# Pooling v in three parts, one routing group for the last nine tiles, and routing operations on both sides of the normalisation

## The chip, the cores and the metric

The kernel runs on one core of a Trainium2 chip. The metric is the device time of one execution in microseconds (us). TensorE (PE) multiplies matrices, VectorE (DVE) and ScalarE (ACT) work on elements, GpSimd (POOL) does element work and issues the indirect DMAs, SyncE (SP) issues most other DMAs. Every engine works through its own queue in order.

## The reference

Three layers follow one another. Only the first two touch the change.

```
k_p = mean of k over 8 neighbours;  v_p likewise             # 8 batches, 8 heads, 576 x 64
attn = softmax(q @ k_p.T / 8);  x = attn @ v_p               # x: 4608 tokens x 512
do   = x @ w_skip > 0;  logits = x @ w_gate                  # 8 experts
e    = argmax(logits);  gate = softmax(logits)[e]
out  = x + gate * (relu(x @ w1[e]) @ w2[e])   where do, else x
y    = (h * sigmoid(h)) @ w_out,  h = out @ w_in             # 2048 wide
```

## The kernel before, in words

**Attention** goes over 36 tiles of 128 tokens. A batch has 576 tokens, so two batches make nine tiles and the middle one of the nine belongs to both. `first[b]` is the first tile of batch b: 0, 4, 9, 13, 18, 22, 27, 31. In pass i of the loop the engines get, in the order of the code: the score products of tile i+3 (`products`, tile name `s`), the transposes of the probabilities of tile i+1 (`ptrans`, `pt` and its copy `pts`), the row maxima and exponentials of tile i+3 (`mx` on VectorE, `prb` on ScalarE), the product with v of tile i (`pv`), and the normalisation of tile i (`post`). There is one PSUM tile for `pv`, so the product of tile i+1 can start only when `post` of tile i has read it. `post` is five VectorE operations: `sm` (add), `sm` (reciprocal), `cc`, `x`, `lg`; `x` is the last but one and the last to read the PSUM tile. `lg` holds the router's logits and the skip score; they come out of `pv` as extra columns, since the router's weights are applied to the pooled v in advance.

**Pooling v.** `pool_v(b)` adds the eight neighbours on GpSimd in three additions (1280, 640 and 320 elements per partition; tile names `v`, `v`, `vp`). In passes with i + 2 = first[b] it is called for batch b+1, all three additions in one pass, from b = 1 on. `router1(b+1)` transposes `vp` on TensorE (`vtp`) three passes later, in pass first[b]+1; `values(b+1)` copies it to its place (`vex`) in the same pass, and `router2` applies the router's weights (`cps`) two passes after that.

**Routing** works on groups of tiles. `GROUP` names five: three of nine tiles, one of six (27 to 32) and one of three (33 to 35). When the last tile of a group has been normalised, `route` appends two steps to a list, and each later pass takes one entry from it. `step1` is eight VectorE operations that end with the one-hot choice `roh`, `rohb` and with `sb`. `count` is one TensorE product and one more per tile (`rps`) and reads `rohb`; it stands in TensorE's queue in front of that pass's `pv`. `step2` is nine VectorE operations that end with the slot numbers `ix`. Then one indirect DMA per tile, issued by GpSimd, scatters the token numbers into a list in DRAM (`slots<-consts,ix`). These scatters are paced: at most one is placed at the start of a pass, behind ScalarE's last instruction, and one at its end, behind VectorE's last instruction. The start one is left out in passes before 18 when three or fewer are waiting.

**The order of VectorE's work in a pass.** The code first exhausts the routing step of this pass (`a`), except in the last two passes, then takes four operations of `self.slow` (`keep_one`, sixteen small operations, from pass 30 on), then pools a part of a later batch's k, and then does `post`, taking one leftover operation of `a` after each of its operations. Passes 30 to 33 also subtract a quarter of the first expert's weights (`w1l`).

**After attention** the last group is routed within the first expert unit: `step1`, two blocks of the first product (`hp`), `count`, `step2`, all of the group's scatters at once, then the work list (`units`, small VectorE operations) beside the blocks that follow. GpSimd then reads the whole token list back (`table<-slots`), behind all scatters. VectorE's `taken` (`table<-table,sc`) waits for it; behind `taken` in VectorE's queue stand the copy `xr`, the last `hl` and the low parts of the second half of the first expert's second weights (`w2l`), which TensorE needs from the fifth block of the second product (`yp`) on. The gather of the next unit's tokens waits for `taken` too. A loop over the other units follows, then the third layer.

An order of issue is fixed per engine by the code, with one exception: the scatters are tied only to their own data and to the instruction that paces them, and the planner may put one ahead of an addition of `pool_v` that was written before it; what is written after a scatter on GpSimd stays behind it.

Of the kernel before, what the change touches and what calls it, by code (L numbers as in the profile page):

```python
# [5 lines left out]
F32 = mybir.dt.float32  # L6
# [7 lines left out]
ALU = mybir.AluOpType  # L14
AX = mybir.AxisListType
# [3 lines left out]
P = 128  # L19
B, H, S, D = 8, 8, 576, 64  # L20
# [5 lines left out]
NTILE = NT // P  # L26
CP, NC = 120, 5
# [15 lines left out]
KEYS = {2: (2, 3, 4, 4), 3: (6, 6, 7, 8), 4: (11, 12, 13, 13), 5: (15, 15, 16, 17), 6: (20, 20, 21, 22),  # L43
        7: (24, 24, 25, 26)}
DEEP = 3
LAST = 32
FMIN = float(np.uint32(0x38100000).view(np.float32))
PACE = [3, 3, 3, 3, 1, 0] + [3, 2, 3] * 5
HALF = 6
# [2 lines left out]
ON0, ON1 = 3,0  # L52
OPS = [2, 2, 2, 0, 4, 4]
ORDER = list(range(NT // 512))[::-1]
SLOW = 4
A1, A2, A3 = 8, 12, 12

C_E, C_MV, C_LID, C_WT, C_THR, C_LE, C_UN, C_PK, C_TRI = 0, 2, 13, 49, 57, 153, 217, 241, 265
# [30 lines left out]


GROUP = {}
for _g, (_t0, _n) in enumerate([(0, 9), (9, 9), (18, 9), (27, 6), (33, 3)]):
    GROUP.update({_t0 + _j: (_g, _j, _n) for _j in range(_n)})


# [62 lines left out]
class Kern:  # L158
# [19 lines left out]
    def attention(self, xa, rs, extra):  # L178
        nc, tc, c = self.nc, self.tc, self.c
        self.todo = todo = []  # L180
        self.slow = iter(())
        with tc.tile_pool(name="as", bufs=1) as s1, \
# [16 lines left out]
            q_t, k_t, v_t, st = {}, {}, {}, {}  # L199
# [10 lines left out]
            def loadq(b):  # L210
                q_t[b] = s2.tile([P, 4, S], F32, name=f"q{b}", tag="q", bufs=3)
                nc.sync.dma_start(q_t[b], self.qT[b])
# [11 lines left out]
                    eng.tensor_tensor(k[:, :, :, 0:2], k[:, :, :, 0:2], k[:, :, :, 2:4], ALU.add)  # L224
                    eng.tensor_tensor(kp, k[:, :, :, 0], k[:, :, :, 1], ALU.add)

            def pool_v(b, on_dve=0):

                v, g, n = v_t.pop(b), nc.gpsimd, on_dve
                vp = st[b, "v"] = s2.tile([P, NC, D], F32, name=f"vp_{b}", tag="vp")  # L230
                if n:
                    nc.vector.tensor_reduce(vp[:CP, 0:n], v[:CP, 0:n].rearrange("p c t d -> p c d t"), AX.X, ALU.add)
                v, vp = v[:CP, n:], vp[:CP, n:]
                g.tensor_tensor(v[:, :, 0:4], v[:, :, 0:4], v[:, :, 4:8], ALU.add)
                g.tensor_tensor(v[:, :, 0:2], v[:, :, 0:2], v[:, :, 2:4], ALU.add)
                g.tensor_tensor(vp, v[:, :, 0], v[:, :, 1], ALU.add)

            def values(b):
                vp, ve = st[b, "v"], vex[b % NB]
# [44 lines left out]
            def products(t):  # L284
                pss = []
                for a in range(2):
                    ps = bank(f"s_{t}{a}")
                    for b, o, r, m in parts(t):
                        for hp in range(2):
                            nc.tensor.matmul(ps[r:r + m, 144 * hp:144 * hp + 144], q_t[b][:, 2 * a + hp, o:o + m],  # L290
                                             kbd[b % NB][:, 2 * a + hp].rearrange("p a g -> p (a g)"),
                                             start=True, stop=True)
                    pss.append(ps)
                return pss
# [60 lines left out]
            first = [9 * (b // 2) + 4 * (b % 2) for b in range(B)]  # L355
# [27 lines left out]
            for i in range(-2, NTILE):  # L383
                if i == -2:
                    pool_v(0, ON0)
                if i > DEEP and i + 3 < NTILE:
                    pss = products(i + 3)
                    pts[i + 1] = ptrans(i + 1, prs.pop(i + 1))
                    prs[i + 3] = scores(i + 3, pss)
                elif i != -1 and i <= DEEP:  # L390
                    prs[i + 2] = scores(i + 2)
                if len(self.to_place) > (3 if i < EARLY else 0) and i < NTILE - 1:
                    self.place(1, nc.scalar.last)
                extra(i, True)
                ready = todo.pop(0) if todo and i < NTILE - 1 else None
                if ready and ready[0]:
                    ready[0]()
                if i == -2:
                    values(0)
                    loadv(1)  # L400
                    loadq(1)
                if i == -1:
                    pss = products(1)
                    router1(0)
                if i == 0:
                    pv(0, pts.pop(0))
                if 0 <= i + 1 < NTILE and i + 1 not in pts:
                    pts[i + 1] = ptrans(i + 1, prs.pop(i + 1))
                if i == -1:
                    prs[1] = scores(1, pss)  # L410
                    router2(0)
                    pool_k(1, nc.vector, (0,))
                    pool_v(1, ON1)
                    values(1)
                if i > 0:
                    pv(i, pts.pop(i))
                a = ready[1]() if ready and ready[1] else iter(())
                b = post(i) if i >= 0 else iter(())
                for _ in range(99 if i < LAST else ready[2] if ready and i < NTILE - 2 else 0):
                    next(a, None)  # L420
                for _ in range(SLOW):
                    next(self.slow, None)
                for bb, tiles in KEYS.items():
                    for r, t in enumerate(tiles):
                        if i == t:
                            pool_k(bb, nc.vector, (r,), 1)
                for _ in b:
                    next(a, None)
                for _ in a:
                    pass  # L430
                for bb, tiles in KEYS.items():
                    if i == tiles[-1]:
                        keys(bb)
                if i == 0:
                    pool_k(1, nc.vector, (2,))
                    keys(1)
                for b in range(B):
                    if i + 4 == first[b] and 0 < b < B - 1:
                        loadq(b + 1)
                    if i + 2 == first[b]:  # L440
                        if 0 < b < B - 1:
                            pool_v(b + 1)
                        if b + 2 < B:
                            loadk(b + 2)
                            loadv(b + 2)
                    if i + 2 == first[b] + 3 + (b == 0) and b + 1 < B:
                        router1(b + 1)
                    if i + 2 == first[b] + 3 and 0 < b < B - 1:
                        values(b + 1)
                    if i + 2 == first[b] + 5 and b + 1 < B:  # L450
                        router2(b + 1)
                if i == DEEP:
                    prs[i + 3] = scores(i + 3)
                if i == EARLY + 7:
                    self.read_table(nc.sync)
                if i == 2:
                    nc.sync.dma_start(self.cb, self.con[:, P + C_TRI:])
                if i == 6:
                    self.consts()
                if i < NTILE - 1:  # L460
                    self.place(1, nc.vector.last)
                else:
                    self.place(len(self.to_place))
                extra(i)
# [1174 lines left out]
```

## Time and profile before

| | |
|---|---|
| time, median of 3 runs | 1295.41 us (1293.82 to 1295.55) |
| the profiled execution: its time, its span | 1300.88 us, 1299.1 us |
| TensorE, VectorE, ScalarE, GpSimd busy in the span | 96%, 66%, 44%, 27% |
| attention (score products to last `pv`) | about 9.7 to 152.2 us |
| first expert unit (first `hp` to last `yp`) | 152.8 to 193.8 us |

The profile was taken from one execution; its span runs from the first to the last instruction. A row of a timeline gives the start and the duration in us, the engine, the code line (a helper's, so the same in all rows), the operation, output <- inputs by tile names, the shape and the count; in square brackets stands the idle time of the engine before it and what ended that. A pass is found by its `pv`.

### The profile page before, as it was taken

Reading aid. Unit: us, or ns where it says so; the run is one execution under the profiler, and the core shown is the slowest. Engines: PE = TensorE matmul, PEld = TensorE weight load, DVE = VectorE, ACT = ScalarE, POOL = GpSimd, SP = SyncE. Lnnn points to the kernel's source line nnn. Section 1 sums busy time; section 2 is a strip of 40 time slices with the busy share of each in tenths; the row PEclk is TensorE's granted clock in tenths of the full one; section 3 lists DMA queues with packets and bytes.
Section 4 is the critical chain, followed back from the end, with each engine's and each line's share of the span. In section 5 each row is a group of like instructions: output and inputs, shape, how many; then the busy total and the mean of one; then the engine's idle time right before and its main releaser. Section 6 shows DMA issues by size and latency. Waiting matters only on the chain.

```text
span 1299.1 us, 20276 instructions
## 1 busy us (share of the span) xinstructions
PE 1244.8 (96%) x6469; PEld 1059.0 (82%) x6470; DVE 851.4 (66%) x1559; ACT 576.7 (44%) x1224; POOL 352.9 (27%) x313
## 2 busy tenths in 40 slices
PE   6998887999989989999999999999999999999998
PEld 5988767998878979887788888788888888888887
DVE  5887785666776768888724245556784657847565
ACT  5877534445565445443433334424344243533321
POOL 5476532122222212212456502111111010210100
PEclk9999998999999999999999999999999999999999
DMA  9887526565565633347664323553546343463532
GB/s 379 302 302 266 195 82 221 176 208 185 209 208 186 232 107 123 138 165 265 235 214 159 130 90 117 199 176 124 167 163 213 131 169 119 155 214 113 178 114 90
DMA packets 94187, 234.43 MB, mean 180 GB/s; under 512 B 15077, under 2 KB 26981, under 8 KB 90400
## 3 DMA queue, kind: packets, MB, share of 16 engines
q1 hardware_dynamic: 86816, 216.47, 48.2%
q0 software_dynamic: 7008, 16.80, 4.0%
q8 instruction: 42, 0.69, 0.2%
q14 instruction: 33, 0.27, 0.1%
q10 hardware_dynamic: 288, 0.20, 0.0%
HBM read 183.24 MB, written 52.89 MB: 182 GB/s over the span
## 4 chain that ended last, share of the span: by engine, by line
PE 60%; DVE 1%; issue 1%; DMA 1%; ACT 0%; SPq 0%; DVEq 0%; ACTq 0%
PE yb L115 21%; PE ps L115 17%; PE fh L115 9%; PE fop L115 9%; PE hp L115 1%; PE yp L115 1%; PE fxp L115 1%; DMA wout<-wdo 0%; DVE fr L115 0%; PE sx L115 0%; DVE ft L115 0%; DVE fsg L115 0%; DMA out<-fo 0%; ACT fgh L115 0%; DVE fgl L115 0%
## 5 line engine op out<-in xcount | busy, mean ns | idle before, releaser
L115 PE MATMUL yb<-wout,g 128*128 128x512 f32 x1152 | 268.4, 391 | 0.8 <-DMA wout<-wdo 0.8
L115 PEld LDWEIGHTS yb<-wout,g 128*128 128x128 f32 x1152 | 215.0, 188 | 45.7 <-DMA wout<-wdo 0.9
L115 POOL TENSOR_TENSOR tm<-tm,tm 128x512 f32<-128x512 f32 x24 | 32.2, 1343 | 411.9 <-ACT tm L115 411.9
L115 DVE TENSOR_TENSOR yacc<-yb,yacc 128x512 f32<-128x512 f32 x168 | 116.1, 691 | 38.7 <-PE yb L115 31.4
L115 ACT COPY tm<-ps 128x512 f32<-128x512 f32 x72 | 42.4, 589 | 146.2 <-PE ps L115 144.4
L115 ACT CAST g<-sg 128x512 fp32r<-128x512 f32 x96 | 59.6, 620 | 76.9 <-DVE sg L115 76.9
L115 DVE TENSOR_TENSOR fsg<-fh,fsg 128x512 f32<-128x512 f32 x48 | 33.1, 689 | 85.7 <-ACT fsg L115 85.7
L115 ACT ACTIVATE hh<-hp 128x256 fp32r<-128x256 f32 (+1 forms) x96 | 39.4, 411 | 105.8 <-PE hp L115 97.2
L115 DVE TENSOR_TENSOR w2l<-raw,w2h 128x512 fp32r<-128x512 f32 x96 | 65.9, 692 | 28.9 <-ACT w2h L115 23.9
L115 PE MATMUL hp<-xth,w1h 128*128 128x256 f32 (+2 forms) x384 | 72.9, 313 | 12.1 <-issue 8.3
L115 PE MATMUL yp<-w2l,hh 128*128 128x512 f32 x208 | 81.2, 390 | 3.0 <-DVE w2l L115 3.0
L115 PE MATMUL fh<-w1l,fh 128*128 128x512 f32 x336 | 83.4, 390 | 0.0
L115 PE MATMUL yp<-w2h,hh 128*128 128x512 f32 x208 | 83.3, 400 | 0.0
L115 PE MATMUL yp<-w2h,hl 128*128 128x512 f32 x208 | 81.3, 391 | 0.0
L115 DVE TENSOR_TENSOR tm<-ps,tm 128x512 f32<-128x512 f32 x24 | 16.6, 691 | 98.1 <-PE ps L115 98.1
L115 PE MATMUL hp<-xtl,w1h 128*128 128x256 f32 (+2 forms) x384 | 72.3, 309 | 2.0 <-DVE xtl L115 1.9
L115 PEld LDWEIGHTS fh<-w1l,fh 128*128 128x128 f32 x336 | 62.8, 188 | 12.9
L115 PEld LDWEIGHTS hp<-xth,w1h 128*128 128x128 f32 x384 | 61.1, 195 | 14.0 <-issue 12.9
L115 PE MATMUL hp<-xth,w1l 128*128 128x256 f32 (+2 forms) x384 | 71.3, 308 | 0.0
L115 ACT ACTIVATE prb<-s,mx 128x72 f32<-128x72 f32 x288 | 65.6, 357 | 9.5 <-DVE mx L115 9.3
L115 PE MATMUL fop<-fh,fgh 128*128 128x512 f32 x168 | 66.4, 395 | 3.2 <-ACT fgh L115 3.2
L115 ACT ACTIVATE fsg<-fh 128x512 f32<-128x512 f32 x48 | 28.7, 599 | 91.6 <-PE fh L115 91.6
(240 smaller groups left out, 2756.2 us busy)
## 6 DMA issues: line engine op xcount, KB each, us to landing
raw<-w SPq DMA_DIRECT2D x88, 512.0 KB
wout<-wdo SPq DMA_DIRECT2D x48, 512.0 KB
win<-wdi SPq DMA_DIRECT2D x36, 512.0 KB
w1l<-wdi SPq DMA_DIRECT2D x36, 512.0 KB
xa<-x SPq DMA_DIRECT2D x36, 256.0 KB
fx<-xa SPq DMA_DIRECT2D x9, 1024.0 KB
v<-vR SPq DMA_DIRECT2D x7, 1280.0 KB
fr<-w_in SPq DMA_DIRECT2D x16, 512.0 KB
```

The lines of the kernel that those rows point to most:

```text
L115: ins = f(*a, **k)
```

## The change

The last nine tiles (27 to 35) become one routing group. `pool_v(b+1)` does one of its three additions in each of the passes first[b]-2, first[b]-1 and first[b], instead of all in the first of them. In every pass five operations of the routing step are issued ahead of the k pooling and of `post`, and the rest of them after `post`. `self.slow` gives two operations in a pass instead of four, and four in the last two passes.

```diff
-LAST = 32
+FILL = 5
-SLOW = 4
+SLOW = 2
-for _g, (_t0, _n) in enumerate([(0, 9), (9, 9), (18, 9), (27, 6), (33, 3)]):
+for _g, (_t0, _n) in enumerate([(0, 9), (9, 9), (18, 9), (27, 9)]):
...
-            def pool_v(b, on_dve=0):
-
-                v, g, n = v_t.pop(b), nc.gpsimd, on_dve
-                vp = st[b, "v"] = s2.tile([P, NC, D], F32, name=f"vp_{b}", tag="vp")
-                if n:
-                    nc.vector.tensor_reduce(vp[:CP, 0:n], v[:CP, 0:n].rearrange("p c t d -> p c d t"), AX.X, ALU.add)
+            def pool_v(b, on_dve=0, steps=(0, 1, 2)):
+                v, g, n = v_t[b], nc.gpsimd, on_dve
+                vp = st.get((b, "v"))
+                if vp is None:
+                    vp = st[b, "v"] = s2.tile([P, NC, D], F32, name=f"vp_{b}", tag="vp")
+                    if n:
+                        nc.vector.tensor_reduce(vp[:CP, 0:n], v[:CP, 0:n].rearrange("p c t d -> p c d t"), AX.X,
+                                                ALU.add)
                 v, vp = v[:CP, n:], vp[:CP, n:]
-                g.tensor_tensor(v[:, :, 0:4], v[:, :, 0:4], v[:, :, 4:8], ALU.add)
-                g.tensor_tensor(v[:, :, 0:2], v[:, :, 0:2], v[:, :, 2:4], ALU.add)
-                g.tensor_tensor(vp, v[:, :, 0], v[:, :, 1], ALU.add)
+                for j in steps:
+                    if j < 2:
+                        m = 4 >> j
+                        g.tensor_tensor(v[:, :, 0:m], v[:, :, 0:m], v[:, :, m:2 * m], ALU.add)
+                    else:
+                        g.tensor_tensor(vp, v[:, :, 0], v[:, :, 1], ALU.add)
...
-                for _ in range(99 if i < LAST else ready[2] if ready and i < NTILE - 2 else 0):
+                for _ in range(FILL):
                     next(a, None)
-                for _ in range(SLOW):
+                for _ in range(SLOW if i < NTILE - 2 else 2 * SLOW):
                     next(self.slow, None)
...
                 for _ in b:
-                    next(a, None)
+                    pass
                 for _ in a:
                     pass
...
+                    if 0 <= i + 2 - first[b] < 3 and 0 < b < B - 1:
+                        pool_v(b + 1, 0, (i + 2 - first[b],))
                     if i + 2 == first[b]:
-                        if 0 < b < B - 1:
-                            pool_v(b + 1)
                         if b + 2 < B:
```

## Rows read from the trace of the kernel before

**Rows 1.** The page: busy time (share of the span) and instructions of each engine.
```profile
PE 1244.8 (96%) x6469; PEld 1059.0 (82%) x6470; DVE 851.4 (66%) x1559; ACT 576.7 (44%) x1224; POOL 352.9 (27%) x313
```
**Rows 2.** Windows, passes 28 to 33: length, busy us (instructions) by engine, clock, DMA share, GB/s.
```profile
122.00:147.00 25.00, 20.82 (x171) 18.73 (x169) 23.52 (x94) 18.70 (x66) 13.99 (x16) 1.00 0.72 239
```
**Rows 3.** Waits of TensorE from 15 to 154 us: total, times, longest.
```profile
PE pv L115 <- DVE x L115: 7.6, 10, 2.1
```
**Rows 4.** Timeline of TensorE: the products with v of tiles 33, 34, 35.
```profile
143.08 1.63 PE L115 MATMUL pv<-vex,pts 120*128 120x148 f32 x10 [1.65 <-DVE x L115]
...
147.46 1.63 PE L115 MATMUL pv<-vex,pts 120*128 120x148 f32 x10 [0.84 <-DVE x L115]
...
150.65 1.61 PE L115 MATMUL pv<-vex,pts 120*64 120x148 f32 x20 [0.91 <-DVE ri L115]
```
**Rows 5.** Timeline of VectorE, passes 30 and 33: slow operations, routing step 1, start of normalisation.
```profile
133.25 0.15 DVE L115 TENSOR_TENSOR sc<-m,tot 1x8 f32<-1x8 f32 x1
...
133.71 0.15 DVE L115 TENSOR_SCALAR sm<-pv 128x8 f32<-128x8 f32 x1
...
144.17 0.20 DVE L115 TENSOR_REDUCE rmx<-lg 128x6 f32<-128x48 f32 x1
...
146.06 0.15 DVE L115 TENSOR_SCALAR sm<-pv 128x8 f32<-128x8 f32 x1
```
**Rows 6.** Timeline of VectorE, passes 18 and 19: a group of nine.
```profile
86.64 0.25 DVE L115 TENSOR_TENSOR roh<-req,rm 128x72 f32<-128x72 f32 x1
...
87.16 0.16 DVE L115 TENSOR_SCALAR sm<-pv 128x8 f32<-128x8 f32 x1
...
88.52 0.82 DVE L115 TENSOR_REDUCE mx<-s 128x4 f32<-128x288 f32 x2
89.25 0.16 DVE L115 TENSOR_TENSOR tot<-tot,rps 128x8 f32<-128x8 f32 x1
...
90.90 0.16 DVE L115 TENSOR_SCALAR sm<-pv 128x8 f32<-128x8 f32 x1
```
**Rows 7.** Timeline of TensorE, pass 19: the count and the product behind it.
```profile
87.67 0.38 PE L115 MATMUL rps<-rohb,onesb 128*128 128x72 bf16 x9
88.57 1.63 PE L115 MATMUL pv<-vex,pts 120*128 120x148 f32 x10 [0.52 <-DVE x L115]
```
**Rows 8.** Timeline of GpSimd, pooling v of batch 4.
```profile
63.12 2.94 POOL L115 TENSOR_TENSOR v<-v 120x1280 f32<-120x1280 f32 x1
66.22 1.00 POOL L115 DMA_INDIRECT slots<-consts,ix  x1 [0.17 <-DVE vex L115]
...
68.88 0.87 POOL L115 TENSOR_TENSOR vp<-v 120x320 f32<-120x320 f32 x1
```
**Rows 9.** Timeline of TensorE, pass 14: the transposes that read this `vp`.
```profile
71.45 0.47 PE L115 MATMUL vtp<-ident,vp 120*128 120x120 f32 x3
```
**Rows 10.** Timeline of GpSimd after attention: scatters and the table read.
```profile
163.49 0.98 POOL L115 DMA_INDIRECT slots<-consts,ix  x1 [4.00 <-DVE ix L115]
164.77 0.98 POOL L115 DMA_INDIRECT slots<-consts,ix  x1 [0.30 <-issue]
...
168.72 0.60 POOL L115 DMA_DIRECT2D table<-slots  x1 [1.68 <-DMA slots<-consts,ix]
```
**Rows 11.** Timeline of VectorE after attention.
```profile
161.05 0.56 DVE L115 SCALAR_TENSOR_TENSOR hl<-hp,hh 128x384 fp32r<-128x384 f32 x1 [3.69 <-ACT hh L115]
...
174.41 0.17 DVE L115 TENSOR_TENSOR sc<-table,m 128x24 f32<-128x24 f32 x1
```
**Rows 12.** Windows: the last stretch in which the table's bytes move; a later half-clock stretch.
```profile
482.60:486.40 3.80, 3.80 (x12) 3.80 (x13) 3.31 (x5) 1.71 (x2) 1.25 (x1) 0.50 0.20 74
...
170.50:171.00 0.50, 0.50 (x4) 0.28 (x2) 0.46 (x3) 0.04 (x1) 0.00 (x0) 1.00 0.18 65
```
**Rows 13.** Timeline of TensorE: two products behind a wait.
```profile
177.24 0.50 PE L115 MATMUL yp<-w2l,hh 128*128 128x512 f32 x1 [1.82 <-DVE w2l L115]
...
482.55 1.62 PE L115 MATMUL hp<-xth,w1h 128*128 128x384 f32 x4 [3.81 <-PEq L1635]
```

## The prediction

> **What bounds the kernel now.** I read the page first: TensorE is busy for 96% of the span [rows 1], so a microsecond counts only where TensorE waits or is pushed back. The change lies in the first 195 us, so I went on with the waits of TensorE over attention. What the reader sees there is that it waits mostly for one thing, the normalisation `x` of the tile before: 7.6 us in ten waits [rows 3]. The windows by stage show why at the end of attention: from 122 to 147 us VectorE is busy 23.5 of 25 us and TensorE 20.8 [rows 2], so there VectorE sets the pace, while before that TensorE does. The timelines of TensorE, VectorE and GpSimd then give the places, and I followed the first expert unit up to the loop. There TensorE waits twice for VectorE's low parts `w2l`, the second time 1.82 us [rows 13], behind VectorE's table work. All sums below are differences within the profiled execution (1300.88 us, span 1299.1); I add them to the median of the plain runs, 1295.41 us, which is 5.5 us lower than the profiled one.
>
> **Part 1: the last tiles lose a routing group.** Four slow operations take 0.46 us before the normalisation (133.25 to 133.71) [rows 5]. Two instead of four save 0.23 us in each of passes 30, 31 and 32, where VectorE is full [rows 2], so tile 33's product starts some 0.7 us earlier, at 142.4 instead of 143.08 [rows 4]. In pass 33 step 1 of the six-tile group and four slow operations lie from 144.17 to 146.06, 1.89 us, ahead of the normalisation [rows 5]; of that 0.23 stays. Then what is late next is TensorE: product, normalisation, product. That cycle is 3.19 us between tiles 34 and 35 (147.46 to 150.65), where step 2 was interleaved with it [rows 4]; without step 2 I put it at 3.1, against 4.38 from tile 33 to tile 34. Tile 34 comes at 145.5 and tile 35 at 148.5, 2.1 us earlier than now, and step 2's end no longer delays the last split of x, which adds a little: **-2.3 us** when the expert unit starts. Bounds: -1.4 (step 1's own 1.89 less 0.46) and -2.9 (0.7 and the whole 2.2 of the two shorter cycles). The eight slow operations that move to passes 34 and 35 cost nothing while VectorE waits there for the product; without that cover they cost 0.5 us a pass. One of two logit stores leaves SP's queue and the other grows to nine tiles; the weight loads behind it are first read after the table's arrival, so I count nothing, and 0.5 us if they came late.
>
> **Part 2: routing operations on both sides of the normalisation.** Five operations of step 1 now come first, and `roh`, `rohb` and `sb` after the normalisation. In pass 18 these three take 0.52 us (86.64 to 87.16) and the normalisation 1.36 us (87.16 to 88.52) [rows 6]. So `x` is ready 0.5 us earlier, but `rohb` only at 88.5 instead of before 87.2. The count reads it, takes 0.38 us, and stands in TensorE's queue in front of the product of tile 19 [rows 7]. Behind that waiting count are this product and the whole next pass. The count would run from 88.6 to 89.0, the product start there instead of at 88.57: 0.4 us later where it should have been 0.5 us earlier. In the next pass four of step 2's nine operations (1.65 us in all, 89.25 to 90.90 [rows 6]) move behind the normalisation, which pays about a third of this back. I count +0.25 and +0.3 us for the first two groups and nothing for the third, which lies where VectorE is full and the order doesn't change its sum: **+0.55 us**. Bounds: -1.6 (the third part of 7.6 us that stands in routing passes outside the tail, an estimate from [rows 3] of two waits a group) and +1.2 (three counts late by 0.4).
>
> **Part 3: v in three parts.** GpSimd runs its queue in order, and in passes with paced scatters a part that is written after a scatter stays behind it. Now one scatter lies between the first addition (63.12) and the end of `vp` (69.75) [rows 8]. With the additions in passes 11, 12 and 13, four lie between: the end of pass 11, start and end of pass 12, start of pass 13. A scatter takes 1.28 us from start to start (163.49 to 164.77) [rows 10]; three more are 3.85 us, and `vp` is ready at 73.6. The transposes that read it stand in TensorE's queue at 71.45 [rows 9]: 2.2 us too early. Behind them wait the next tile's scores and everything after. The same pattern stands a second time, with batch 6 in pass 23; the other four batches are pooled where no scatter is waiting. A mean wait for `x` is 0.76 us [rows 3], and one such wait at each place is swallowed by the late start, so I take 2.2 - 0.76 = 1.45 twice: **+2.9 us**. Bounds: 0, if the planner lets the additions go ahead or GpSimd is early, and +5.0, if nothing is swallowed and the scatters of pass 13 wait for their pacer a little longer. What GpSimd has gained by then (scatters that come out earlier) nobody waits for.
>
> **Part 4: nine scatters after attention instead of three.** The scatters follow `ix`, one every 1.28 us, and the table read waits for the last: 168.72 us [rows 10]. Six more are 7.7 us. A count of ten products instead of four adds 0.25 us; step 2 on nine tiles takes 1.65 us [rows 6], and with three it fills 161.6 to the first scatter at 163.49 less its latency, about 1.6, so it adds nothing. The table's bytes have moved by 171.0 [rows 12], and VectorE takes the table at 174.4 without a wait [rows 11]; allowing 0.4 us for the signal, 3.0 us of the delay are hidden. Left are 7.7 + 0.3 - 3.0 = **+5.0 us**. Behind the waiting VectorE operation stand the copy `xr`, which the next unit's gather waits for, the last `hl`, and the four `w2l` that TensorE already waits for at 177.24 [rows 13]; from there to the loop VectorE's chain has no room of that size, and the loop starts from its end. Bounds: +2.6, if the 3.69 us in which VectorE waited before 161.05 [rows 11] shrink to what the count then sets (2.4 us less), and +8.0, if the signal came only just in time.
>
> **Part 5: the clock in that wait.** TensorE's wait before the fifth block grows from 1.82 us [rows 13] to nearly 7. [...] From the rows I take about half, **+1.0 us**, since VectorE's own chain runs on beside those products and the adds wait for it; bounds 0 and +1.9.
>
> **Sum:** -2.3 + 0.55 + 2.9 + 5.0 + 1.0 = +7.15, and 1295.41 + 7.15 = **1302.6 us**.
>
> **The rivals.** A: the v parts are in time (the planner orders the scatters late). For it: in the rows a scatter was put ahead of an addition, so the order is the planner's; against: what is written after a scatter can't pass it. Then +4.25, 1299.7 us. B: the 3.69 us gap of VectorE doesn't come back, so the scatters start 2.4 us earlier. For it: TensorE's block that ScalarE waited for had long ended; against: nothing of the change lies in it. Then +4.75, 1300.2 us; with A as well, 1297.3. C, the other side: the normalisation's lead takes away every wait of TensorE for `x`, 7.6 us [rows 3], in place of parts 1 and 2, with v in time. Against the 6.0 us of parts 4 and 5 that leaves -1.6, 1293.8 us, faster or the same. It decides from 6 us of waits on. For it: it is the largest wait of the stage; against: the longest, 2.1 us, is behind a pooling of k, which stays ahead of the normalisation, and the count needs what is put behind it.
>
> **How the numbers follow.** A change of 0.2%, 2.6 us, is about what a measurement of this kernel can tell from none. Chances: the forecast 0.50, A 0.20, B 0.12 (with or without A), C 0.10, something else 0.08. Slower by over 2.6 us: 0.47 of the forecast, 0.15 of A, 0.09 of B and 0.03 of the rest, 0.74. Within: 0.03, 0.05, 0.03, 0.06 of C and 0.03, 0.20. Faster: 0.06. The likeliest case's own range, with the bounds of its parts, is 1299.5 to 1305.5; the range for all is 1297.0 to 1306.0, which leaves out C and the far ends.
>
> **What would show it.** Right: nine scatters in a row after attention, the table read some 5 to 6 us later behind the first `hp`, and TensorE idle near 7 us inside the first `yp` block, followed by a clock of 0.5; transposes `vtp` that wait for `vp` in passes 14 and 23; counts that wait for `rohb`; tiles 33 to 35 at 3.1 us each. Wrong: `vtp` without a wait (A), first scatter within 2 us of the count (B), or tiles before 122 us closer together than now (C). The prediction fails as a whole if VectorE reaches `taken` and finds the table there.

## The result and the profile after

The changed kernel takes 1305.4 us (median of 6), the kernel before 1296.0 beside it: ratio 1.0087, 95% interval 1.0070 to 1.0104. That is 9.4 us slower by the medians and some 11 by the ratio. The side was right; 1302.6 was too little. The profiled execution took 1309.89 us, span 1307.8, and was the slowest of the six. TensorE is busy 4.1 us more than in [rows 1], but only 0.8 more than in a second trace of the kernel before (e5 below: 1248.1 us busy, span 1291.8), while the span is 16.0 longer than there. Against that trace nearly all of the loss is waiting:
```profile
PE 1248.9 (95%) x6468; PEld 1063.5 (81%) x6469; DVE 851.1 (65%) x1542; ACT 577.6 (44%) x1224; POOL 356.5 (27%) x313
```
Attention first. Timelines of TensorE and GpSimd, after: the transposes of the pooled `v`, four scatters inside the pooling [rows 8, 9], the counts behind `rohb` [rows 7], and the last three tiles 3.08 us apart [rows 4]. The waits for `x` fall from 7.6 us in ten [rows 3] to 3.5 in four (in e5 they are 4.9 in eight).
```profile
74.96 0.53 PE L115 MATMUL vtp<-ident,vp 120*128 120x120 f32 x3 [2.20 <-POOL vp L115]
108.69 0.53 PE L115 MATMUL vtp<-ident,vp 120*128 120x120 f32 x3 [1.54 <-POOL vp L115]
...
57.14 0.21 PE L115 MATMUL rps<-rohb,trib 128*128 128x72 bf16 x1 [0.43 <-DVE rohb L115]
90.87 0.21 PE L115 MATMUL rps<-rohb,trib 128*128 128x72 bf16 x1 [0.55 <-DVE rohb L115]
128.82 0.19 PE L115 MATMUL rps<-rohb,trib 128*128 128x72 bf16 x1 [1.37 <-DVE rohb L115]
...
143.54 1.63 PE L115 MATMUL pv<-vex,pts 120*128 120x148 f32 x10 [1.12 <-DVE x L115]
146.62 1.63 PE L115 MATMUL pv<-vex,pts 120*128 120x148 f32 x10 [0.91 <-DVE x L115]
```
```profile
64.61 2.93 POOL L115 TENSOR_TENSOR v<-v 120x1280 f32<-120x1280 f32 x1
67.70 0.99 POOL L115 DMA_INDIRECT slots<-consts,ix  x1 [0.17 <-issue]
...
73.03 0.99 POOL L115 DMA_INDIRECT slots<-consts,ix  x1 [0.30 <-ACT prb L115]
74.01 0.90 POOL L115 TENSOR_TENSOR vp<-v 120x320 f32<-120x320 f32 x1
```
Then the tail. GpSimd after: nine scatters, the eighth 3.27 us long, and the table read [rows 10].
```profile
160.17 0.98 POOL L115 DMA_INDIRECT slots<-consts,ix  x1 [7.03 <-DVE ix L115]
161.46 0.98 POOL L115 DMA_INDIRECT slots<-consts,ix  x1 [0.30 <-issue]
...
169.16 3.27 POOL L115 DMA_INDIRECT slots<-consts,ix  x1 [0.30 <-issue]
172.74 0.98 POOL L115 DMA_INDIRECT slots<-consts,ix  x1 [0.30 <-issue]
175.41 0.60 POOL L115 DMA_DIRECT2D table<-slots  x1 [1.69 <-DMA slots<-consts,ix]
```
VectorE after [rows 11]: its subtractions stand beside that scatter, and it now waits for the table.
```profile
169.10 2.48 DVE L115 TENSOR_TENSOR w2l<-raw,w2h 128x512 fp32r<-128x512 f32 x4
...
177.91 0.18 DVE L115 TENSOR_TENSOR table<-table,sc 128x24 f32<-128x24 f32 x1 [5.89 <-DMA table<-slots]
```
TensorE after [rows 13]: the wait for `w2l`, the wait ahead of the loop's first product (8.26 us in the trace read before the prediction), and the one at its exit; then windows with the granted clock [rows 12].
```profile
180.59 0.80 PE L115 MATMUL yp<-w2l,hh 128*128 128x512 f32 x1 [7.74 <-DVE w2l L115]
208.51 1.27 PE L115 MATMUL hp<-xth,w1h 128*128 128x256 f32 x4 [10.19 <-issue]
491.03 1.62 PE L115 MATMUL hp<-xth,w1h 128*128 128x384 f32 x4 [6.00 <-PEq L1640]
```
```profile
182.10:186.30 4.20, 4.20 (x11) 3.25 (x10) 2.99 (x18) 1.24 (x2) 1.01 (x1) 0.50 0.60 162
186.30:192.00 5.70, 5.70 (x30) 4.78 (x28) 5.38 (x7) 1.19 (x2) 0.39 (x1) 0.99 0.00 0
```
The traces of the chips on which the kernel before takes 1293 to 1296 us, side by side, in us, worked out from the timelines. Attention: first product with v to the first product of the first expert unit (the "first FFN product" of the expectations). Table, last: from that product to VectorE's second operation on the table, and to the end of the unit's last product. Entry: TensorE's wait ahead of the loop's first product. Loads: start of the loads for the fourth block of the third layer (the "fourth FFN block" of the expectations), ahead of the last product's end. The traces of e9 to e16, from two other chips, follow with their experiments.
```
                     attention  table  last   entry  loads
before (rows 1-13)    133.9    21.8   41.0    8.3    1.5
before again (e5)     131.1    20.2   39.5    6.2    1.5
after                 131.6    26.0   46.5   10.2    3.2
after again (e1)      133.2    26.2   46.7   10.9    3.2
after again (e17)     133.2    26.1   45.2    6.8    1.8
group only (e2)       128.3    26.1   46.4   10.1    3.0
parts only (e3)       134.3    20.2   39.7    5.8    1.5
order only (e4)       131.8    20.3   39.6    7.1    1.5
six in the tail (e6)  133.1    20.1   39.5    6.1    1.5
sub ahead (e7)        131.5    28.1   46.9    7.4    1.5
sub behind (e8)       133.2    23.8   45.2    7.0    1.5
late loads (e18)      131.5    26.0   46.3    6.6    1.4
```
The same kernel's attention differs by 1.7 to 2.7 us from trace to trace, so its total can't weigh smaller effects. But product by product these traces agree within 0.05 us over long stretches, so it can be said where a difference lies: the first trace of the kernel before starts tile 28 4.2 us later than e5, counted from the first product with v, and e2, e4 and e6 start it within 0.1 us of e5. The columns table and last repeat within 1.5 us for equal code, but for the first row, which stands apart.

### The profile page after: what moved, and what is told of

It is laid out like the page before. It is cut to its first block, busy times and chain, and to the rows that moved or that the text cites. A ratio compares the mean times of both kernels' runs of the same rounds, so it can differ in the third digit from the quotient of the medians.

```text
span 1307.8 us, 20248 instructions
## 1 busy us (share of the span) xinstructions
PE 1248.9 (95%) x6468; PEld 1063.5 (81%) x6469; DVE 851.1 (65%) x1542; ACT 577.6 (44%) x1224; POOL 356.5 (27%) x313
## 4 chain that ended last, share of the span: by engine, by line
PE 60%; DVE 1%; issue 1%; DMA 1%; ACT 0%; SPq 0%; DVEq 0%; ACTq 0%
PE yb L115 21%; PE ps L115 17%; PE fop L115 10%; PE fh L115 9%; PE hp L115 2%; PE yp L115 1%; PE fxp L115 1%; DMA wout<-wdo 0%; PE sx L115 0%; DVE fsg L115 0%; DVE fr L115 0%; DMA out<-fo 0%; ACT fgh L115 0%; DVE fgl L115 0%; DVE ft L115 0%
## 5 line engine op out<-in xcount | busy, mean ns | idle before, releaser
L115 ACT ACTIVATE hh<-hp 128x256 fp32r<-128x256 f32 (+1 forms) x96 | 39.5, 411 | 108.2 <-PE hp L115 101.7
L115 ACT ACTIVATE prb<-s,mx 128x72 f32<-128x72 f32 x288 | 65.5, 354 | 10.7 <-DVE mx L115 10.7
L115 DVE TENSOR_TENSOR g<-sg,g 128x512 fp32r<-128x512 f32 x96 | 65.8, 686 | 5.4 <-ACT g L115 5.0
```

Source lines behind the costliest of these rows:

```text
L115: ins = f(*a, **k)
```

## The experiments

Ratios are to the kernel before in the same set of runs, with 95% intervals.

**e1, no edit (after).** 

> The changed kernel unaltered, beside the three that follow. Two waits of TensorE that nothing in the diff explains are longer in its trace than in the one before: ahead of the loop's first product (10.19 us against 8.26) and at the loop's exit (6.00 against 3.81), 4.1 us of the 8.7 by which the spans differ. Theory T1 (they belong to the program, or follow from the longer table path): both stand here within 0.3 us of 10.2 and 6.0, and the ratio to the kernel before is 1.0085 to 1.0095. Rival T2 (they vary from execution to execution): at least one is over 1 us nearer to the kernel before's.

1.0085 (1.0062 to 1.0109), entry 10.9, exit 4.95: the entry wait repeats, the exit does not.

**e2, the group alone.**
```diff
-... [(0, 9), (9, 9), (18, 9), (27, 6), (33, 3)]
+... [(0, 9), (9, 9), (18, 9), (27, 9)]
```


> The kernel before with one edit: its last nine tiles are one routing group. T1 (the nine scatters with the table behind them are the main loss): the table is used 3 to 5 us later after the start of the first FFN block than before (15.7 us there: 158.3 to 174.6 less the block's start), the half-clock stretch follows, passes 33 to 35 give back up to 2, and the time is up by 3 to 6 us, ratio 1.0023 to 1.0046. Rival T3 (the order of the routing operations and the late transposes are the main loss): under +1.5 us, ratio below 1.0012. Of the loop's two waits: if they hang on the longer table path they are long here too (10 and 6 us), otherwise about 8.3 and 3.8.

1.0041 (1.0026 to 1.0056), +5.3 us: attention 2.8 shorter, everything behind it worse, the entry long too. Up to tile 33 its products with v start within 0.03 us of e5's; from tile 33 to tile 35 they are 6.15 us apart where e5's are 9.00. T1 holds, T3 falls. TensorE:
```profile
177.09 0.80 PE L115 MATMUL yp<-w2l,hh 128*128 128x512 f32 x1 [7.77 <-DVE w2l L115]
204.72 1.22 PE L115 MATMUL hp<-xth,w1h 128*128 128x256 f32 x4 [10.06 <-issue]
```
**e3, the parts alone** (`pool_v` and its call as in the change). 

> The kernel before with one edit: v pooled in parts in three passes. T1: the transposes of the pooled v in passes 14 and 23 wait for GpSimd's last addition 1.5 to 2.2 us, the net is 0.3 to 1.5 us each, and the time is up by 1 to 3 us, ratio 1.0008 to 1.0023. Rival T3: since the normalisation of before's order keeps those passes short of VectorE anyway, the two waits hide in the waits for x, and the ratio is 0.9995 to 1.0005. The loop's two waits as in the kernel before (8.3 and 3.8 us) if they hang on the table path.

1.0017 (1.0001 to 1.0032), +2.2 us: T1, though the interval reaches into T3's 0.9995 to 1.0005. The waits stand where they were forecast, and are not hidden: tile 28 starts 4.6 us later than in e5.
```profile
73.90 0.53 PE L115 MATMUL vtp<-ident,vp 120*128 120x120 f32 x3 [1.89 <-POOL vp L115]
109.18 0.53 PE L115 MATMUL vtp<-ident,vp 120*128 120x120 f32 x3 [1.54 <-POOL vp L115]
```
**e4, the order alone** (`FILL = 5`, `SLOW = 2` and the loops that use them). 

> The kernel before with one edit: five routing operations ahead of the normalisation in every pass and the rest behind it, two of the one-row operations in place of four. T1: the waits of the value products for x in passes 10, 11, 19, 20 go (about -0.5 us each), waits of the count products for rohb come (0.4 to 1.4 us), passes 33 to 35 lose less to the one-row operations (up to -1.5 us), and the time moves by -2 to +1 us, ratio 0.9985 to 1.0008. Rival T3 (the order is the main loss): over +2 us, ratio above 1.0015.

1.0001 (0.9989 to 1.0012): T1; the order by itself costs nothing measurable.

**e5, no edit (before).** 

> The kernel before unaltered, for a second trace of it: the execution whose trace was read took 1300.88 us, 5 above the median. Theory T5 (those 5 us lie in the gaps of passes 14 to 25 and at the loop's entry, and are of that execution): here the stretch from the first value product to the first product of the FFN is 1.5 to 4 us shorter than the 133.85 read, the wait ahead of the loop's first product is 5.8 to 7.1 us as in the two kernels with one edit and three tail scatters, and the span is 1293 to 1296. Rival T6 (they are the program's, and the edits take them away): 133.9, 8.3 and 1299.

1.0000 (0.9987 to 1.0013), span 1291.8. T5 holds with 131.1 and 6.2; the span is a little under its 1293. The 3.69 us gap of VectorE [rows 11] belonged to that execution too: here the first scatter comes 8.4 us after the first FFN product, in the changed kernel 8.3, in the trace of rows 10 10.7. The tail is compared with this trace from here on. GpSimd and TensorE:
```profile
159.45 0.98 POOL L115 DMA_INDIRECT slots<-consts,ix  x1 [1.71 <-DVE ix L115]
...
166.57 0.60 POOL L115 DMA_DIRECT2D table<-slots  x1 [3.56 <-DMA slots<-consts,ix]
```
```profile
173.93 0.50 PE L115 MATMUL yp<-w2l,hh 128*128 128x512 f32 x1 [1.73 <-DVE w2l L115]
196.77 1.22 PE L115 MATMUL hp<-xth,w1h 128*128 128x256 f32 x4 [6.24 <-issue]
```
**e6, six in the tail.**
```diff
-... (18, 9), (27, 6), (33, 3)]
+... (18, 9), (27, 3), (30, 6)]
```


> The kernel before with its last nine tiles as groups of three and six: six scatters in the tail in place of three or nine, five groups as before. T1 with a threshold (the table path counts only from where it outlasts the products): the scatters end some 6 us earlier after the first FFN product than with nine, before the eighth's place beside the four subtractions, the table is used 19.5 to 21 us after the first FFN product (20.3 with three, 26.1 with nine), TensorE's wait for w2l stays at 1 to 2 us, the full clock holds and the entry wait is 6 to 8: ratio 0.999 to 1.001. Rival T7 (every scatter more in the tail costs the same, a sixth of what six cost): half of the 9 to 10 us of tail and entry that nine cost over three, +4.5 us, ratio 1.0035.

1.0013 (1.0000 to 1.0025). Table 20.1, last 39.5, wait for `w2l` 1.71: three more scatters cost the tail nothing, six more cost 7 us. It is a threshold, T7 falls. The trace's loss lies in attention, where the waits for `x` are 8.7 us in all against 4.9 in e5, the longest 3.3 in front of tile 33's product.

**e7, subtractions ahead of the table** (in the changed kernel).
```diff
+mm1(U * P, (7,), False)
+for f in range(4, 8):
+    low2(f)
 self.taken()
...
-mm1(U * P, (7,), False)
-for f in range(4, 8):
-    low2(f)
```


> The changed kernel with the last four subtractions of the second weights' low part, and the FFN block that they need, issued ahead of the two operations on the table. T1 (the table's lateness costs by way of VectorE, which stands at the table with those subtractions behind it): TensorE's wait of 7.7 us ahead of the fifth block's low product and the half clock behind it go, the last product of the stage ends 7 to 9 us earlier after the first FFN product than 46.5, the entry wait falls to 6 to 8 us, and the time falls to 1295 to 1299, ratio 0.999 to 1.0025. Rival T8 (the gather behind the table is what counts): the wait moves to the transposes of the gathered rows and 4 us or more of it stay, ratio above 1.005. More of VectorE's subtractions stand beside the scatters here: if those lengthen them (T4), more than one scatter is longer than 1.2 us.

1.0074 (1.0054 to 1.0094): T8, not T1. The wait for `w2l` goes (0.21 us), and the gathered rows are late in its place, 5.3 and 0.9 us; and now two scatters are long. GpSimd, VectorE and TensorE:
```profile
168.94 3.27 POOL L115 DMA_INDIRECT slots<-consts,ix  x1 [0.30 <-issue]
172.52 2.94 POOL L115 DMA_INDIRECT slots<-consts,ix  x1 [0.31 <-issue]
```
```profile
168.88 2.48 DVE L115 TENSOR_TENSOR w2l<-raw,w2h 128x512 fp32r<-128x512 f32 x4
172.10 2.47 DVE L115 TENSOR_TENSOR w2l<-raw,w2h 128x512 fp32r<-128x512 f32 x4
```
```profile
186.35 0.48 PE L115 MATMUL xtp<-ident,xn 128*128 128x128 f32 x1 [5.31 <-DMA xn<-xa,gi]
```
**e8, subtractions behind the table** (in the changed kernel).
```diff
-for f in range(4):
-    low2(f)
 ...
 self.taken()
+for f in range(4):
+    low2(f)
```


> The changed kernel with the first four of those subtractions moved behind the table's two operations, so that no subtraction stands beside the scatters. T4 (a VectorE operation with two inputs lengthens the scatter that it meets): the eighth scatter takes 0.98 us instead of 3.27 and the table is used 2.0 to 2.4 us earlier (23.7 to 24.1 us after the first FFN product instead of 26.1). Rival T9 (the eighth scatter is long for a reason of its own, such as the number of scatters under way): it stays at 3.2 us. TensorE is the worse for it in either case, since it stands from the first block's low product on: 2 to 3 us of products that ran ahead of the wait now run behind it, so that under T4 the time is within 1 us of the changed kernel's, ratio to before 1.0075 to 1.0095, and under T9 2 to 3 us above.

1.0060 (1.0040 to 1.0081). T4 holds: the eighth scatter takes 0.98 us and the table comes 2.3 us earlier. The time was better than T4's 1.0075; the entry wait is short in this trace (7.0 us), which may be why.
```profile
169.70 0.98 POOL L115 DMA_INDIRECT slots<-consts,ix  x1 [0.30 <-issue]
170.99 0.98 POOL L115 DMA_INDIRECT slots<-consts,ix  x1 [0.30 <-issue]
```
e9 to e16 ran on two other chips, where the kernel before takes 1300.7 and 1301.9 us.

**e9, e10, e12: groups of 9, 9, 12 and 6** (`(18, 12), (30, 6)`, two tiles widened), in the kernel before, in the changed one, and in the kernel before with the new order. 

> The kernel before with four routing groups of 9, 9, 12 and 6 tiles in place of five of 9, 9, 9, 6 and 3: one group fewer, as in the change, but six scatters in the tail, which cost the table nothing. T1: the table is used 20 to 20.5 us after the first FFN product, the last product of the stage ends at 39.5 and the entry wait is 6 to 7, all as in the kernel before; the attention from the first value product on is 1 to 2.8 us shorter than 131.1 (128.3 with 9, 9, 9 and 9); ratio 0.9978 to 0.9992. Rival T11 (the twelve scatters of the third group and the one-row operations behind it, all in the last six passes, take that back there): attention 131 to 133, ratio 1.000 to 1.0015.

> The changed kernel with groups of 9, 9, 12 and 6 tiles in place of 9, 9, 9 and 9: the parts of v and the order of the routing operations stay, six scatters stand in the tail in place of nine. T1 (the nine scatters carry the loss, in the tail and at the loop's entry): TensorE waits 1.7 us for w2l in place of 7.7, the last product ends 39.5 us after the first FFN product in place of 46.5, the entry wait is 6 to 7 in place of 10 to 11, and 10 us of the 11 go: ratio 0.999 to 1.0025. Rival T3 (order and parts together cost more than each by itself): ratio above 1.004.

> The kernel before with groups of 9, 9, 12 and 6 tiles and with the changed order of the routing operations, v pooled whole. T1: as the run with the groups alone, and the order moves it by -1 to +1 us (it was +0.1 us by itself, interval -1.4 to +1.6); with two one-row operations to a pass in place of four, those behind the third group run on into the FFN and lie behind VectorE's first work there: ratio 0.998 to 0.9998. Rival T11: above 1.0005, with TensorE's waits for x in passes 31 to 35 over 4 us in all.

1.0045 (1.0030 to 1.0060), 1.0032 (1.0018 to 1.0045), 1.0047 (1.0032 to 1.0063). None gains. In e9 and e12 T11 has the side right, but its size is far off: attention is 141.5 us in e9 where it said 131 to 133, while the waits for `x` in e12's passes 31 to 35 are 3.5 us where it said over 4. How much of that is the third group's work in the last passes isn't shown, for in all three traces ScalarE also stands 5.0 to 5.7 us there, and TensorE 2.9 to 3.1, for a releaser that the profile calls remote. TensorE of e9:
```profile
157.90 2.34 PE L115 MATMUL pv<-vex,pts 120*64 120x148 f32 x20 [2.92 <-remote]
```
In e10 the waits for `w2l` are down to 0.6 and 1.8 and the entry to 7.3, as T1 has it, but attention is 137.5, and the ratio lies between T1's 1.0025 and T3's 1.004, with an interval that reaches into both.

**e11, a quarter of the loads.**
```diff
-self.load_w1(e)
+nc.sync.dma_start(self.raw1[:, 0], self.row(self.w1, e)[0:P, :])
```


> The changed kernel, with three of the four loads of an expert's first weights left out at the top of the loop (the loop's units compute with rows that are not the expert's). Only the wait ahead of the loop's first product is read. T10 (an instruction fetch stands behind those loads in the DMA queues, since they start 0.6 us behind the stage's last product there and the fetch comes behind them): with a quarter of the bytes the wait falls from 10.2 to 10.9 us to 4 to 7. Rival T12 (the fetch is late by itself, whatever the loads): 9.5 us or more.

One run. The entry was 7.18 us, but the wait for `w2l` was 4.81 for another reason (below), and other kernels with whole loads have 7 there too: inconclusive.

**e13, the fourth block's loads late.**
```diff
-self.ffn_load(3)
...
+self.xtrans((2, 3))
+self.ffn_load(3, behind=nc.vector.last)
```


> The changed kernel with one thing moved: the two loads for the fourth FFN block wait for VectorE's last split of the gathered rows. In the traces with the long entry wait (10.1 to 10.9 us) these loads start 3.0 to 3.2 us ahead of the stage's last product and the first instruction fetch of queue q8 comes 1 to 2 us behind that product; in the traces with a short one (5.8 to 8.3) they start 1.5 us ahead, and the fetch comes 1 to 2 us ahead of the product. T10 (the fetch stands behind those loads in the DMA queues): with the loads at 1.4 to 1.6 us ahead the fetch comes ahead of the product again, the wait falls to 6 to 8 us although TensorE still waits 7.7 us for w2l and the clock is halved, and the time falls by 2 to 4 us against the changed kernel, ratio to before 1.0055 to 1.007. Rival T12 (the fetch is late because TensorE is): the wait stays at 9.5 us or more, ratio 1.008 to 1.0095.

0.9986 (0.9968 to 1.0004), outside the ranges of both theories, with a wait for `w2l` of 4.82 us, so it did not tell T10 from T12. It showed something else: ScalarE stands still ahead of the last blocks, VectorE's subtractions come behind the scatters, and no scatter is lengthened. ScalarE, VectorE and GpSimd:
```profile
174.45 0.49 ACT L115 ACTIVATE hh<-hp 128x384 fp32r<-128x384 f32 x1 [4.07 <-remote]
```
```profile
175.45 2.49 DVE L115 TENSOR_TENSOR w2l<-raw,w2h 128x512 fp32r<-128x512 f32 x4
```
```profile
170.43 0.98 POOL L115 DMA_INDIRECT slots<-consts,ix  x1 [0.30 <-issue]
171.72 0.98 POOL L115 DMA_INDIRECT slots<-consts,ix  x1 [0.30 <-issue]
```
**e14 (the changed kernel with the old groups) and e15 (with v whole).** 

> The changed kernel with the nine last tiles as groups of six and three again: the parts of v and the order stay. T1 (the nine scatters carry the loss): the tail and the entry are those of the kernel before (39.5 us and 6 to 8 us), the parts cost 2 to 3 us and the order 0 to 1 in the attention: ratio 1.001 to 1.003. Rival T3 (order and parts together cost more than each by itself): 1.004 or more.

> The changed kernel with v pooled whole again: the group of nine and the order stay. T1: tail and entry as in the changed kernel (46.5 and 10 to 11 us), no wait of the transposes for the pooled v, the attention 2 to 3 us shorter than 132.4 (the mean of five traces with the parts): ratio 1.0055 to 1.0075. Rival T13 (the transposes' waits are hidden): 1.0085.

1.0008 (0.9992 to 1.0024) and 1.0000 (0.9980 to 1.0020). e14 fits T1 loosely; e15 misses it: the group and the order, +0.4% in e2 and e4 together, cost nothing on this chip.

**e16, e7's edit in the kernel before.** 

> The kernel before with the last four subtractions and the FFN block that they need issued ahead of the two operations on the table, as was done to the changed kernel. T1: TensorE's wait of 1.7 us for w2l goes (0.0 to 0.3), the table is used 2.5 to 4 us later after the first FFN product than 20.2, and whether the gathered rows are still in time decides: if they are, the last product ends 37.5 to 38.2 us after the first in place of 39.5 and the ratio is 0.9985 to 0.9995. Rival T8 (the gather is what counts here too): TensorE waits over 1.5 us at the transposes of the gathered rows, ratio 1.000 or more.

1.0011 (0.9993 to 1.0029): no gain. The second wait for `w2l` falls to 0.18 us, and transposes wait 1.3 us in all for the rows and 3.4 for their own splits: T8. Up to the tail this is the kernel before, so its attention, 136.2 us against 133.8 in e13, is the kernel before's on this chip. The loads start 4.2 us ahead of the last product's end here, and the entry wait is the shortest of all:
```profile
204.40 1.22 PE L115 MATMUL hp<-xth,w1h 128*128 128x256 f32 x4 [2.91 <-DVE xr L115]
```
**e17 (after, a third time) and e18 (e13's kernel) on one more chip,** the kernel before at 1292.7. 

> The changed kernel unaltered. The runs so far fall into two kinds of place: on two chips the kernel before takes 1294 us, on two others 1301 to 1302, and there kernels with nine scatters show two gaps of ScalarE of 2 to 5.6 us in the FFN ahead of the fifth to eighth block, after which VectorE's subtractions come behind the scatters, the eighth scatter is not lengthened, TensorE waits 4.8 us for w2l in place of 7.7 and the entry wait is 7.2 to 7.5. T14 (how much the change costs depends on the chip by way of these gaps): where the kernel before takes 1293 to 1296 here, the ratio is 1.007 to 1.010 with a wait for w2l of 7.7 and an entry of 10 to 11; where it takes 1300 to 1302, the ratio is 0.999 to 1.0035 with 4.8 and 7 to 8. Rival T15 (the two kinds are chance, the change costs the same everywhere): ratio 1.006 or more with either.

> The changed kernel with the loads for the fourth FFN block waiting for VectorE's last split, on the same chip as the changed kernel itself. Where TensorE waits 7.7 us for w2l there: by T10 (the fetch stands behind those loads) the entry wait falls from 10 to 11 us to 6 to 8 and the time by 2 to 4 us, by T12 both stay. Where it waits 4.8 us there: the loads start 1.5 us ahead of the last product anyway, and the two kernels agree in both waits and within 0.15% in time by either theory.

1.0086 (1.0064 to 1.0109) and 1.0083 (1.0061 to 1.0105). The kernel of e13, 0.9986 there, is at 1.0083 here: what the change costs depends on the chip, as T14 says and T15 denies, shown with that near twin; the changed kernel itself was not run on a 1301 us chip. T14's way, the gaps of ScalarE, is one part of it. With them the nine scatters cost the first expert unit 2.2 us on e13's chip (its last product ends 44.0 us after its first begins in e13 and e15, 41.8 in e14) where they cost 7 elsewhere. The other part is attention, where kernels with v whole are late there without the parts: they start tile 28 104.9 to 109.2 us after the first product with v (e9, e12, e15, e16), against 100.4 to 100.5 in e2, e4, e5 and e6, and the kernels with the parts at 103.6 to 105.4 on either kind of chip. Why is open. The entry wait was expected long in e17 and was 6.8, with the loads 1.8 us ahead: T10 and T12 stay undecided. TensorE and a window of e17:
```profile
181.33 0.79 PE L115 MATMUL yp<-w2l,hh 128*128 128x512 f32 x1 [7.78 <-DVE w2l L115]
204.54 1.22 PE L115 MATMUL hp<-xth,w1h 128*128 128x256 f32 x4 [6.78 <-issue]
```
```profile
182.70:184.40 1.70, 1.70 (x5) 1.31 (x4) 1.60 (x8) 0.00 (x0) 1.14 (x2) 0.52 0.73 186
184.50:190.00 5.50, 5.50 (x26) 4.55 (x25) 4.31 (x12) 1.23 (x2) 0.00 (x0) 1.00 0.22 61
```
No version beat the kernel before beyond its interval.

## Why the prediction was right on the side and short in size

- **Part 1 (-2.3): right.** Attention is 2.8 us shorter in e2 than in e5, all of it behind tile 33; the tiles stand 3.08 us apart where 3.1 was said. Tile 33 itself gains 0.3 us from tile 30 on where 0.7 was said.
- **Part 2 (+0.55): within its bounds.** e4 gives +0.1 us (-1.4 to +1.6). Waits for `x` went and counts wait for `rohb`, as said; the third group's count, put at nothing, waits 1.37 us, and in e4 tile 33 starts with e5's all the same.
- **Part 3 (+2.9): right in mechanism, within its bounds in size.** e3 gives +2.2 us (0.1 to 4.1); four scatters lie in the pooling, the first wait is the 2.2 us forecast, the second 1.5. Rival A is out. That a wait for `x` swallows a third of each isn't seen: the traces with the parts start tile 28 3.1 to 4.9 us later than e5, where 2.9 was said. The first trace of the kernel before stands 4.2 us behind e5 there too, with v whole, so not all executions have this to lose. That these parts cost more and the last tiles gain more than forecast (3.1 us against e5, with part 1's 0.3), so that attention as a whole comes out (+0.4 to +2.1 us against e5, +1.15 forecast), is luck.
- **Part 4 (+5.0): right in mechanism, 0.8 us small.** Against e5 the table is read 8.0 us later and used 5.8 later; 2.2 are hidden (against the trace of the rows it is used 4.2 later). The 8.0 are six scatters (7.7), one lengthened by 2.3 that the sum did not have, less 1.9 of the wait between last scatter and table read (3.56 to 1.69). The 0.4 us for the signal was the author's allowance; in after the table's bytes have moved by 177.5 us and VectorE takes it at 177.91. The lengthening could have been read from the trace before, where a scatter of the last passes meets a subtraction of `w1l`. GpSimd and VectorE, before:
```profile
143.12 1.99 POOL L115 DMA_INDIRECT slots<-consts,ix  x1 [0.30 <-ACT pts L115]
```
```profile
143.04 1.21 DVE L115 TENSOR_TENSOR w1l<-raw,w1h 128x1024 fp32r<-128x1024 f32 x1
```
- **Part 5 (+1.0): within its bounds.** The last product moves by 5.8 to 7.2 us against the table's 5.8 to 6.0: nothing is lost behind the table in e17, 1.0 to 1.3 us in after, e1 and e2. That this is the clock is argued from the windows above, not isolated. No run shows the +1.0 itself; what they show in its place is a granted clock of 0.50 behind the wait of 7.74 us in after, up to 186.3 us, and of 0.52 behind that of 7.78 in e17, up to 184.4.
- **Rival B** was no effect of the change: the 3.69 us gap is missing in e5 as well.
- **The step that failed** is the end of part 4: "the loop starts from its end". It puts the change of TensorE's wait ahead of the loop's first product at nothing, without a reason. In the traces of after, e1 and e2 that wait is 3.8 to 4.7 us longer than in e5. In e17, where it is 0.5 longer, the span is 7.2 us above e5's (1299.0 less 1291.8), which is the sum of 7.15, in part by chance, since the two traces come from two chips. The sum thus lacks 2 to 4 of the 9 to 11 us. The edits one by one (e2, e3, e4) lack nearly as much: they add up to 7.6 us, each known to some 2 us. How much of it the entry wait carries in a median execution isn't shown: the traces of after and e1 took 4.5 us more than the median of their runs, that of e17 3.2 less. The exit wait (6.0, 4.95 and 3.7 us in three traces of one kernel) is not the change's. The range was narrow besides: the parts' own bounds add up to -1.9 and +14.7 us, the range for all allowed +1.6 to +10.6.

What makes the entry long is open. In the three traces with 10 to 11 us the block's loads start 3.0 to 3.2 us ahead of the last product's end, in those with 5.8 to 8.3 us 1.4 to 1.8; but in e16 they start 4.2 us ahead, and the wait is 2.9. DMA packets of after by queue, 194.0 to 199.3 us (no instruction packets) and 199.3 to 200.3, the last product ending at 198.3:
```profile
q1 hardware_dynamic: 641, 0.97, 54.5%
q0 software_dynamic: 2, 0.00, 0.0%
```
```profile
q8 instruction: 1, 0.02, 5.9%
```
In e17 that packet starts between 196.8 and 197.8, ahead of the last product's end at 197.8. The packets of this queue place the wait: in all 20 traces the loop's first product starts 2.7 to 3.4 us behind the second of them that follows the start of the loads. The first of them starts 0.2 to 1.0 us behind the loads, e16's too, but 4.5 to 4.6 us behind them in after, e1 and e2. So early loads alone don't make the wait long. A fetch that stands behind the loads (T10) fits after, e1 and e2; so does one that is late as TensorE is (T12). Whether the packets of q8 are the fetch of the loop's instructions, no run here shows.

## What to carry to other kernels

Work taken off a stage that waits little can come back whole in the tail, where nothing covers it: ask how many microseconds the covering work still lasts, and count to that threshold (six scatters cost the tail nothing, nine cost 7 us). Follow a delay past the end of the stage to the wait ahead of the next one, and take a second trace of the kernel before when the first is 5 us off its median: product by product the two show where the 5 us lie. A loss of 0.8% on one chip can be none on another, as with e13's kernel: compare on more than one.

## What the runs showed of the hardware

- A scatter that GpSimd starts while VectorE runs subtractions of `w2l` or `w1l`, which have both inputs in SBUF, ends 0.85 to 0.89 us after the last of them, whatever its own 0.98 us (after: 172.43 against 171.58; e7: 172.21 and 175.46 against 171.36 and 174.57; before: 145.11 against 144.25). All 30 such scatters of the 20 traces do; with the subtractions moved the eighth takes 0.98 (e8). The 14 that start beside `xtl<-xtp,xth`, one input of which TensorE has just written to PSUM, take 0.98, though up to 0.8 us of it is left. What makes the difference isn't shown: the two kinds of subtraction differ in shape too (128x512 and 128x1024 against 128x384).
- On the chips where the kernel before takes 1301 us, ScalarE stood up to 6.8 us (e14) in the first unit with a releaser that the profile calls remote, which no trace of the chips at 1293 to 1296 us shows. Its cause is open.
- After a like wait of 7.7 to 7.8 us the granted clock stayed at half (0.50 to 0.52) to 186.3 us in after, 5.7 us on, and to 184.4 in e17, 3.1 us on, in the same kernel.
